# Order of the steps in the first rounds: weight split, gate split, masks, scores

## The chip, the cores and the metric

The kernel runs on one core of a Trainium2 chip. The metric is the device time of one execution in microseconds (us), the median of several runs. PE is TensorE, DVE is VectorE, ACT is ScalarE, POOL is GpSimd, SP is SyncE, which issues most DMAs here.

## The reference

A linear attention with per-channel decay over r, k, v of shape (4, 8, 768, 48) gives x of shape (3072, 384). On x stands a mixture of 8 experts, whose gate is balanced by 8 rounds of row and column normalisation, and whose outputs are summed densely.

```python
for t in range(S):                                   # attention
    cur = einsum('bhd,bhe->bhde', u * kt, vt)
    y[:, :, t] = einsum('bhd,bhde->bhe', rt, state + cur)
    state = w[..., None] * state + einsum('bhd,bhe->bhde', kt, vt)
x = y.transpose(0, 2, 1, 3).reshape(3072, 384)
P = exp(x @ w_gate - max)                            # gate, then 8 times:
P /= P.sum(1) ; P /= P.sum(0) ; P *= N / E
out = sum_e P[:, e] * (relu(x @ w1[e]) @ w2[e])
```

## The kernel before

The tokens are 24 tiles of 128. The attention takes a tile per *round* (loop over i, line 720, 27 rounds), as a pipeline: `prep(i + 2)` scales r on POOL and k on DVE by decay tables; `bonus_dot(i + 1)` forms r k u on POOL; `stage_b(i + 1)` transposes r and k on PE, with two ACT copies; `bonus(i)` is a DVE sum and two POOL products; `stage_c(i)` makes the scores pA, which DVE copies through a mask into at_ (two buffers whose masked half stays zero), and the state update pu; `stage_e(i - 2)` transposes x, which ACT has scaled, casts it to f16 on ACT and takes the f16 residue on DVE, both into hbx; `stage_d(i - 1)` multiplies the masked scores with v (py), after which DVE makes x, its maximum and a power-of-two scale; `stage_f(i - 3)` multiplies x by the split gate matrix (px). The PSUM pool ps3, tag pa, has four buffers in turn for the transposes, pA, pu and py of all these.

Every f32 operand of the experts becomes two f16 parts, a high part (ACT) and a low part, the residue (DVE). Expert 0's products (`g1_unit`, `g2_half`, in the list units) run on PE between the stages from round 5 on, by `work` at two places of a round. In rounds 0 to 4 `work` calls `spin(3)`, three matmuls on zeros, instead. Experts 1 to 7 follow after the loop.

Expert 0's weights are split in the rounds too. `split_weights` (line 151) gives a list of steps for w1 and then for w2: three maxima `amax`, `reduce_max`, an empty step, `across` (maximum over partitions by PE), an empty step, `scale`, then `high` and `low` for three chunks. `prepare()` runs the next step; STEPS (line 708) tells how many of them a round runs at its two places: the first (a) follows `stage_c`, the second (b) follows `stage_d`. The gate matrix wg is split likewise by `gate_max`, `gate_across` and `gate_split`, all three in round 2. Each engine keeps the order in which the program issues its instructions (class InOrder).

Ahead of the rounds stand the fills (hbx, at_, wbd, rp, kp), the decay tables on DVE, and an If (line 409) on a flag from DVE, whose body runs only for decays out of range. SP issues the loads in program order; the loads of v 1, r 3, k 3, wg, v 2 and v 3 stand behind the If (lines 413 to 418).

Of the kernel before, what the change touches and what calls it, by code (L numbers as in the profile page):

```python
# [8 lines left out]
F32 = mybir.dt.float32  # L9
# [3 lines left out]
ALU = mybir.AluOpType  # L13
# [19 lines left out]
def rwkv_sinkhorn_moe(  # L33
# [13 lines left out]
    V, S_, G, T, Q = (  # L47
        InOrder(tc, e) for e in (nc.vector, nc.scalar, nc.gpsimd, nc.tensor, nc.sync)
    )
# [4 lines left out]
    P = 128  # L54
# [96 lines left out]
    def split_weights(e, r1, r2, home):  # L151
        w1h = part(home, F16, 0, (KC, F))
        w1l = part(home, F16, KC * F, (KC, F))
        w2h = part(home, F16, 2 * KC * F, (FC, DM))
        w2l = part(home, F16, 2 * KC * F + FC * DM, (FC, DM))
        isw = const.tile([P, 2], F32, name=f"isw_{e}")
        sw = sm.tile([P, 2], F32, tag="sw", name=f"sw_{e}")
        m = sm.tile([P, 2 * KC], F32, tag="wm", name=f"wm_{e}")
        ma_ = [sm.tile([P, 1], F32, tag=f"wma{j}", name=f"wma_{e}_{j}") for j in range(2)]
        res = {}  # L160
        pieces = []

        def rest_():
            pass

        for raw, wh, wl, j in ((r1, w1h, w1l, 0), (r2, w2h, w2l, 1)):
            fl = [x.rearrange("p c f -> p (c f)") for x in (raw, wh, wl)]
            n = fl[0].shape[1] // KC

            def amax(i, fl=fl, j=j, n=n):  # L170
                V.tensor_reduce(
                    m[:, j * KC + i : j * KC + i + 1], fl[0][:, i * n : (i + 1) * n],
                    axis=AX.X, op=ALU.max, apply_absolute_value=True,
                )

            def reduce_max(j=j):
                V.tensor_reduce(ma_[j], m[:, j * KC : (j + 1) * KC], axis=AX.X, op=ALU.max)

            def across(j=j):
                res[j] = over_partitions(ma_[j], 1, ps1, "ph", f"w{e}_{j}")  # L180
                next(res[j])

            def scale(j=j):
                pow2_scale(next(res[j]), isw[:, j : j + 1], sw[:, j : j + 1], 0.25)

            def high(i, fl=fl, j=j, n=n):
                sl = slice(i * n, (i + 1) * n)
                S_.activation(fl[1][:, sl], fl[0][:, sl], AF.Copy, scale=sw[:, j : j + 1])

            def low(i, fl=fl, j=j, n=n):  # L190
                sl = slice(i * n, (i + 1) * n)
                V.scalar_tensor_tensor(
                    fl[2][:, sl], fl[0][:, sl], sw[:, j : j + 1], fl[1][:, sl],
                    op0=ALU.mult, op1=ALU.subtract,
                )

            steps = [lambda i=i, f=amax: f(i) for i in range(KC)] + [reduce_max, rest_, across, rest_, scale]
            for i in range(KC + 1):
                fs = [lambda i=i, f=high: f(i)] if i < KC else []
                fs += [lambda i=i, f=low: f(i - 1)] if i else []  # L200
                if i >= KC - 1:
                    fs.append(lambda i=i, j=j: split_done.add((("w1", "w2")[j], i - KC + 1)))
                steps.append(lambda fs=fs: [f() for f in fs])
            pieces += steps
        return (w1h, w1l, w2h, w2l, isw), pieces
# [113 lines left out]
    for c in range(KC):  # L319
# [11 lines left out]
    V.memset(unit[:, :, 0:1], 1.0)  # L331
    V.memset(step[:, :, 0:1], 0.0)
    V.memset(hbx[:, HB : 2 * HB], 0.0)
    S_.mul(
        hbx[:, 2 * HB :].rearrange("p (a q) -> p a q", q=HP),
        unit[:, :1, 1:].broadcast_to([P, HB // HP, HP]), 0.0,
    )
    spin(19)
    wbd = ac.tile([P, NPAIR, 2, D], F32, name="wbd")
    G.memset(wbd, 0.0)  # L340
# [11 lines left out]
    at_ = [ac.tile([P, H, C], F32, name=f"at{i}") for i in range(2)]  # L352
    for t_ in rp_ + kp_:
        G.memset(t_[:, :, D:], 0.0)
    for t_ in at_:
        G.memset(t_, 0.0)

    wlim = part(hb3, F32, 2496, (H, D))[:1]
    flag = ac.tile([1, 1], F32, name="flag")
# [51 lines left out]
            scan_channels(scratch)  # L411

    load_part(1, "v", v)
    load_part(3, "r", r)
    load_part(3, "k", k)
    Q.dma_start(wg, w_gate.rearrange("(c p) e -> p c e", p=P))
    load_part(2, "v", v)
    load_part(3, "v", v)

# [14 lines left out]
    V.tensor_tensor(tab[:, :, HP:], pw[:, :, :HP], gb, op=ALU.mult)  # L434
    V.tensor_tensor(tab[:, :, :HP], iv[:, :, HP:0:-1], gb, op=ALU.mult)
    S_.copy(tabr[:, :, :HP], pw[:, :, HP - 1 :: -1])
    S_.copy(tabr[:, :, HP:], iv[:, :, 1:])
    rtab = ac.tile([P, NPAIR, 2, HP], F32, name="rtab")
    ktab = ac.tile([P, NPAIR, 2, HP], F32, name="ktab")
# [42 lines left out]

    def bonus_dot(tt):
        ld_ = loads[tt]
        rk = at2.tile([P, H, D], F32, tag="rk", name=f"rk_{tt}", bufs=3)
        G.tensor_tensor(rk, ld_["r"], ld_["k"], op=ALU.mult)
        G.tensor_tensor(rk, rk, ub, op=ALU.mult)
        st[tt]["rk"] = rk

# [213 lines left out]
    for sg in range(3):  # L703
# [2 lines left out]
        side += steps  # L706

    STEPS = {
        0: (2, 1), 1: (1, 2), 2: (2, 1), 3: (1, 1), 4: (1, 0),
        5: (1, 1), 6: (2, 2), 7: (3, 1), 8: (1, 1),  # L710
    }

    def n_steps(i):
        return STEPS.get(i, (2, 2) if i < 22 else (3, 2))
# [3 lines left out]
    stage_b(0)  # L718
    bonus_dot(0)
    for i in range(NTT + 3):  # L720
        if i == 2:
            gate_max()
        if i + 2 < NTT:
            if i + 4 < NTT:
                load_chunk(i + 4)
            if i == 0:
                Q.dma_start(raws[1], w2[0].rearrange("(c p) d -> p c d", p=P))
            prep(i + 2)
        if i + 1 < NTT:
            bonus_dot(i + 1)  # L730
            stage_b(i + 1)
        if 2 <= i <= NTT + 1:
            scale_x(i - 2)
        work(1, i > 4)
        if i < NTT:
            bonus(i)
            if ("S", i) in st:
                st[i]["S"] = st.pop(("S", i))
            stage_c(i)
        for _ in range(n_steps(i)[0]):  # L740
            prepare()
        if i <= NTT:
            work(2 if i > 8 else 1, i > 4)
        if i == 2:
            gate_res = gate_across()
        if i >= 2:
            bank_ = ps2.tile([P, TB], F32, tag="po", name=f"px_{i}")
        if 2 <= i <= NTT + 1:
            stage_e(i - 2, bank_)
            emitted[0] = i - 1  # L750
        if i > NTT:
            work(2)
        if 1 <= i <= NTT:
            stage_d(i - 1)
        if i == 2:
            gate_split(gate_res)
        for _ in range(n_steps(i)[1]):
            prepare()
        if 3 <= i:
            stage_f(i - 3, bank_)  # L760
        done = i - 2
        if 0 <= done < NTT and done % TH == TH - 1:
            po_ = done // TH
            if po_ == 0:
                units += [g1_unit(0, fc, W) for fc in range(FC)]
                units += [g2_half(0, t, 0, W) for t in range(TH)]
                pend = [(0, t, 1) for t in range(TH)]
            for j in range(2 if po_ else 0):
                g1 = [g1_unit(po_, fc, W) for fc in range(j * FHC, (j + 1) * FHC)]
                g2 = [g2_half(*a, W) for a in pend]  # L770
                units += merged(g1, g2)
                pend = [(po_, t, j) for t in range(TH)]
# [447 lines left out]
```

## Time and profile before

| | us |
|---|---|
| median of 3 runs | 1563.85 (1563.62 to 1565.07) |
| the profiled execution | 1563.49 |
| its span, first to last instruction | 1561.8 |
| PE busy | 1549.8 |
| DVE, ACT, POOL busy | 1020.8, 671.9, 589.0 |

The granted clock of PE is 1.000 over the span. Round i of the attention can be found in the trace by PE's `stage_b`: the transposes prT of tile 5 (round 4) start at 43.53 us and the last round ends near 258 us. A busy engine is not an engine at its peak, and an average over the span says little of the first 50 us; so the rows are read round by round. In a timeline, the bracket at the end of a line tells how long the engine stood idle before it and who released it.

### The profile page before, as it was taken

How to read it: one execution, taken by the hardware profiler on the slowest of the kernel's cores; microseconds unless marked ns; L12 is line 12 of the kernel's file. 1: busy time of each engine (PE TensorE's matmuls, PEld its weight loads, DVE VectorE, ACT ScalarE, POOL GpSimd, SP SyncE). 2: the span in 40 equal slices, each digit the busy share in tenths (PEclk: the TensorE clock that was granted, in tenths of full speed). 3: DMA queues.
4: the chain of work that ended last, by engine and by line, in shares of the span. 5: the costliest groups of instructions: out<-in, count | busy, mean ns of one | idle time of the engine just before them, and what ended most of it. 6: DMA issues, size and time to landing. Idle time of an engine off the chain costs nothing.

```text
span 1561.8 us, 24068 instructions
## 1 busy us (share of the span) xinstructions
PE 1549.8 (99%) x9297; PEld 899.0 (58%) x9297; DVE 1020.8 (65%) x1694; ACT 671.9 (43%) x1190; POOL 589.0 (38%) x688
## 2 busy tenths in 40 slices
PE   8999999999999999999999999999999999999999
PEld 5877786655555555555555555555555555555555
DVE  7876674957666676666666666666666656656554
ACT  3433332534444354544444453544444444535320
POOL 8777764620012424243342424242423324242200
PEclk9999999999999999999999999999999999999999
DMA  9333311221215556576766666565545555556434
GB/s 197 68 88 79 84 49 36 98 82 45 92 64 103 79 87 111 85 127 90 128 83 122 86 127 90 93 95 70 86 57 99 57 95 61 96 59 97 56 91 132
DMA packets 167638, 138.26 MB, mean 89 GB/s; under 512 B 90337, under 2 KB 161762, under 8 KB 167522
## 3 DMA queue, kind: packets, MB, share of 16 engines
q0 software_dynamic: 44928, 61.36, 32.6%
q1 hardware_dynamic: 122384, 75.35, 17.4%
q8 instruction: 73, 1.20, 0.3%
q14 instruction: 43, 0.35, 0.1%
q10 hardware_dynamic: 210, 0.00, 0.0%
HBM read 55.39 MB, written 80.23 MB: 87 GB/s over the span
## 4 chain that ended last, share of the span: by engine, by line
PE 95%; DVE 2%; POOL 1%; ACT 0%; issue 0%; DMA 0%; SPq 0%; POOLq 0%; DVEq 0%; ACTq 0%
PE po L29 47%; PE bZ L29 11%; PE bY L29 11%; PE ph L29 5%; PE bA L29 5%; PE bB L29 5%; PE py L29 3%; PE bC L29 2%; PE pA L29 1%; PE pu L29 1%; PE px L29 1%; PE prT L29 1%; POOL rk L29 1%; PE pkT L29 1%; DVE tb L29 0%
## 5 line engine op out<-in xcount | busy, mean ns | idle before, releaser
L29 PE MATMUL po<-ws,hbx 128*128 128x384 f16 x3360 | 736.8, 326 | 0.0
L29 POOL DMA_DIRECT2D accd<-stg x288 | 249.7, 867 | 695.4 <-ACT stg L29 681.1
L29 PEld LDWEIGHTS <-hbx 128*128 128x128 f16 x3504 | 336.3, 98 | 292.7 <-issue 1.3
L29 PEld LDWEIGHTS <-ws 128*128 128x128 f16 x3096 | 302.4, 98 | 243.8 <-issue 1.4
L29 ACT ACTIVATE hbx<-tb 128x512 f16<-128x512 f32 x224 | 141.0, 630 | 450.0 <-DVE tb L29 450.0
L29 PE MATMUL po<-ws,hb 128*128 128x384 f16 x1248 | 322.8, 326 | 0.0
L29 DVE TENSOR_TENSOR tb<-bY,tb 128x512 f32<-128x512 f32 x168 | 116.1, 691 | 195.6 <-PE bY L29 195.4
L29 ACT ACTIVATE stg<-po,pe 128x384 f32<-128x384 f32 x312 | 179.1, 574 | 121.8 <-PE po L29 94.9
L29 PE MATMUL bZ<-xv,ws 128*128 128x512 f16 x840 | 227.0, 379 | 0.4 <-DVE tb L29 0.4
L29 PE MATMUL bY<-xv,ws 128*128 128x512 f16 x840 | 227.0, 379 | 0.0
L29 DVE TENSOR_TENSOR tb<-bZ,tb 128x512 f32<-128x512 f32 x168 | 115.5, 688 | 136.0 <-PE bZ L29 136.0
L29 PEld LDWEIGHTS <-hb 128*128 128x128 f16 x1248 | 121.9, 98 | 93.0
L29 POOL TENSOR_TENSOR ucb<-rawb 128x256 f32<-128x256 f32 x84 | 75.8, 953 | 118.0 <-DMA rawb<-in_moe_w_dram 118.0
L29 DVE TENSOR_TENSOR tb<-bB,tb 128x512 f32<-128x512 f32 x112 | 77.4, 691 | 49.2 <-PE bB L29 47.3
L29 PE MATMUL ph<-hbx,ws 128*128 128x384 f16 x576 | 104.3, 326 | 0.5 <-DVE hb L29 0.5
L29 DVE SCALAR_TENSOR_TENSOR hb<-tb,hbx 128x512 f16<-128x512 f32 x112 | 77.2, 689 | 24.6 <-ACT hbx L29 19.5
L29 PE MATMUL bA<-xv,ws 128*128 128x512 f16 x336 | 90.8, 379 | 0.0
L29 PE MATMUL bB<-xv,ws 128*128 128x512 f16 x336 | 90.8, 379 | 0.0
L29 DVE SCALAR_TENSOR_TENSOR hbx<-tb,hbx 128x512 f16<-128x512 f32 x112 | 77.9, 695 | 14.7 <-ACT hbx L29 10.4
L29 DVE SCALAR_TENSOR_TENSOR hb<-ph,hb 128x384 f16<-128x384 f32 x64 | 35.3, 553 | 40.7 <-ACT hb L29 40.5
L29 ACT COPY tb<-bZ 128x512 f32<-128x512 f32 x56 | 32.7, 585 | 65.6 <-PE bZ L29 65.6
L29 ACT ACTIVATE hb<-ph 128x384 f16<-128x384 f32 x64 | 31.2, 489 | 59.7 <-PE ph L29 58.7
(165 smaller groups left out, 1613.7 us busy)
## 6 DMA issues: line engine op xcount, KB each, us to landing
accd<-stg POOLq DMA_DIRECT2D x288, 192.0 KB, 3.7
rawb<-in_moe_w_dram SPq DMA_DIRECT2D x28, 768.0 KB, 7.1
e0d<-stg SPq DMA_DIRECT2D x48, 192.0 KB, 1.9
hb<-e0d SPq DMA_DIRECT2D x48, 192.0 KB, 3.7
rn<-in_r_dram SPq DMA_DIRECT2D x24, 192.0 KB, 3.2
kn<-in_k_dram SPq DMA_DIRECT2D x24, 192.0 KB, 3.6
vn<-in_v_dram SPq DMA_DIRECT2D x24, 192.0 KB, 2.8
accd<-stg SPq DMA_DIRECT2D x24, 192.0 KB, 1.8
```

Of the source, the lines that this page charges most:

```text
L29: return lambda *a, **k: self.tc.keep_in_program_order(f(*a, **k))
```

## The change

The weight steps are cut anew: two highs stand alone, and each further high comes two steps ahead of its low (14 steps per matrix instead of 12), with other numbers in STEPS. `gate_max` and `gate_across` move from round 2 to round 1, `gate_split` from the end of round 2 to behind its `stage_c`, and wg's load from behind r 3 and k 3 to ahead of them. The two buffers of at_ are filled by ACT (a broadcast multiply by zero, as one part of hbx already was) instead of POOL: the first behind the fill of hbx, the second between the two copies of the table tabr. POOL's product r k of tile 0 (rk0) is issued ahead of the If. In round 0, `stage_b(1)` follows `stage_c(0)` instead of preceding it.

```diff
--- before.py
+++ after.py
@@ -195,11 +195,15 @@
                 )
 
             steps = [lambda i=i, f=amax: f(i) for i in range(KC)] + [reduce_max, rest_, across, rest_, scale]
-            for i in range(KC + 1):
-                fs = [lambda i=i, f=high: f(i)] if i < KC else []
-                fs += [lambda i=i, f=low: f(i - 1)] if i else []
-                if i >= KC - 1:
-                    fs.append(lambda i=i, j=j: split_done.add((("w1", "w2")[j], i - KC + 1)))
+
+            steps += [lambda i=i, f=high: f(i) for i in range(2)]
+            for i in range(KC):
+                fs = [lambda i=i, f=high: f(i + 2)] if i + 2 < KC else []
+                if fs:
+                    steps.append(lambda fs=fs: fs[0]())
+                fs = [lambda i=i, f=low: f(i)]
+                if i:
+                    fs.append(lambda i=i, j=j: split_done.add((("w1", "w2")[j], i - 1)))
                 steps.append(lambda fs=fs: [f() for f in fs])
             pieces += steps
         return (w1h, w1l, w2h, w2l, isw), pieces
@@ -331,10 +335,15 @@
     V.memset(unit[:, :, 0:1], 1.0)
     V.memset(step[:, :, 0:1], 0.0)
     V.memset(hbx[:, HB : 2 * HB], 0.0)
-    S_.mul(
-        hbx[:, 2 * HB :].rearrange("p (a q) -> p a q", q=HP),
-        unit[:, :1, 1:].broadcast_to([P, HB // HP, HP]), 0.0,
-    )
+
+    def fill(x_):
+        n = x_.shape[1]
+        S_.mul(
+            x_.rearrange("p (a q) -> p a q", q=HP),
+            unit[:, :1, 1:].broadcast_to([P, n // HP, HP]), 0.0,
+        )
+
+    fill(hbx[:, 2 * HB :])
     spin(19)
     wbd = ac.tile([P, NPAIR, 2, D], F32, name="wbd")
     G.memset(wbd, 0.0)
@@ -352,8 +361,10 @@
     at_ = [ac.tile([P, H, C], F32, name=f"at{i}") for i in range(2)]
     for t_ in rp_ + kp_:
         G.memset(t_[:, :, D:], 0.0)
-    for t_ in at_:
-        G.memset(t_, 0.0)
+    fill(at_[0].rearrange("p h c -> p (h c)"))
+
+    rk0 = at2.tile([P, H, D], F32, tag="rk", name="rk_0", bufs=3)
+    G.tensor_tensor(rk0, loads[0]["r"], loads[0]["k"], op=ALU.mult)
 
     wlim = part(hb3, F32, 2496, (H, D))[:1]
     flag = ac.tile([1, 1], F32, name="flag")
@@ -411,9 +422,9 @@
             scan_channels(scratch)
 
     load_part(1, "v", v)
+    Q.dma_start(wg, w_gate.rearrange("(c p) e -> p c e", p=P))
     load_part(3, "r", r)
     load_part(3, "k", k)
-    Q.dma_start(wg, w_gate.rearrange("(c p) e -> p c e", p=P))
     load_part(2, "v", v)
     load_part(3, "v", v)
 
@@ -434,6 +445,7 @@
     V.tensor_tensor(tab[:, :, HP:], pw[:, :, :HP], gb, op=ALU.mult)
     V.tensor_tensor(tab[:, :, :HP], iv[:, :, HP:0:-1], gb, op=ALU.mult)
     S_.copy(tabr[:, :, :HP], pw[:, :, HP - 1 :: -1])
+    fill(at_[1].rearrange("p h c -> p (h c)"))
     S_.copy(tabr[:, :, HP:], iv[:, :, 1:])
     rtab = ac.tile([P, NPAIR, 2, HP], F32, name="rtab")
     ktab = ac.tile([P, NPAIR, 2, HP], F32, name="ktab")
@@ -482,8 +494,10 @@
 
     def bonus_dot(tt):
         ld_ = loads[tt]
-        rk = at2.tile([P, H, D], F32, tag="rk", name=f"rk_{tt}", bufs=3)
-        G.tensor_tensor(rk, ld_["r"], ld_["k"], op=ALU.mult)
+        rk = rk0
+        if tt:
+            rk = at2.tile([P, H, D], F32, tag="rk", name=f"rk_{tt}", bufs=3)
+            G.tensor_tensor(rk, ld_["r"], ld_["k"], op=ALU.mult)
         G.tensor_tensor(rk, rk, ub, op=ALU.mult)
         st[tt]["rk"] = rk
 
@@ -706,8 +720,8 @@
         side += steps
 
     STEPS = {
-        0: (2, 1), 1: (1, 2), 2: (2, 1), 3: (1, 1), 4: (1, 0),
-        5: (1, 1), 6: (2, 2), 7: (3, 1), 8: (1, 1),
+        0: (2, 1), 1: (1, 2), 2: (4, 2), 3: (1, 1), 4: (0, 1),
+        5: (1, 1), 6: (1, 2), 7: (4, 2), 8: (1, 1),
     }
 
     def n_steps(i):
@@ -718,7 +732,7 @@
     stage_b(0)
     bonus_dot(0)
     for i in range(NTT + 3):
-        if i == 2:
+        if i == 1:
             gate_max()
         if i + 2 < NTT:
             if i + 4 < NTT:
@@ -728,6 +742,7 @@
             prep(i + 2)
         if i + 1 < NTT:
             bonus_dot(i + 1)
+        if i + 1 < NTT and i:
             stage_b(i + 1)
         if 2 <= i <= NTT + 1:
             scale_x(i - 2)
@@ -737,11 +752,15 @@
             if ("S", i) in st:
                 st[i]["S"] = st.pop(("S", i))
             stage_c(i)
+        if i == 2:
+            gate_split(gate_res)
+        if i == 0:
+            stage_b(1)
         for _ in range(n_steps(i)[0]):
             prepare()
         if i <= NTT:
             work(2 if i > 8 else 1, i > 4)
-        if i == 2:
+        if i == 1:
             gate_res = gate_across()
         if i >= 2:
             bank_ = ps2.tile([P, TB], F32, tag="po", name=f"px_{i}")
@@ -752,8 +771,6 @@
             work(2)
         if 1 <= i <= NTT:
             stage_d(i - 1)
-        if i == 2:
-            gate_split(gate_res)
         for _ in range(n_steps(i)[1]):
             prepare()
         if 3 <= i:

```

## Rows read from the trace of the kernel before

**Rows 1.** The page's table of busy time: engine, busy us, share, instructions.

```profile
PE 1549.8 (99%) x9297; PEld 899.0 (58%) x9297; DVE 1020.8 (65%) x1694; ACT 671.9 (43%) x1190; POOL 589.0 (38%) x688
```

**Rows 2.** PE's waits, 13 to 79 us: engine, tile, releaser, total us, times, longest.

```profile
PE pu L29 <- ACT rT L29: 1.6, 1, 1.6
PE px L29 <- DVE hbx L29: 1.1, 2, 0.8
PE prT L29 <- POOL rp L29: 0.6, 2, 0.5
PE pmax_w L29 <- DVE wma L29: 0.4, 1, 0.4
```

**Rows 3.** Timeline of PE: start us, us, engine, operation, count, [idle before <-releaser].

```profile
16.77 1.16 PE L29 MATMUL pA<-rT,kT 64*128 64x128 f32 x16
...
38.82 1.13 PE L29 MATMUL pu<-vn,kp 128*128 128x96 f32 x8 [1.59 <-ACT rT L29]
...
43.38 0.29 PE L29 MATMUL px<-wgp,hbx 128*128 128x16 f16 x6
...
51.80 0.29 PE L29 MATMUL px<-wgp,hbx 128*128 128x16 f16 x6 [0.81 <-DVE hbx L29]
...
78.19 0.29 PE L29 MATMUL px<-wgp,hbx 128*128 128x16 f16 x6 [0.31 <-DVE hbx L29]
```

**Rows 4.** Timeline of POOL, 0 to 50 us.

```profile
5.90 1.84 POOL L29 MEMSET at<- 128x1024 f32 x2
...
14.97 1.31 POOL L29 TENSOR_TENSOR rk<-rn,kn 128x384 f32<-128x384 f32 x1
```

**Rows 5.** Timeline of ACT, round 7.

```profile
75.56 1.15 ACT L29 ACTIVATE ws<-ws,sw 128x1024 f16<-128x1024 f32 x1 [3.22 <-DVE sw L29]
...
76.61 0.47 ACT L29 ACTIVATE hb<-ph 128x384 f16<-128x384 f32 x1
```

**Rows 6.** Timeline of DVE, around the If.

```profile
6.98 0.78 DVE L29 TENSOR_SCALAR wsafe<-wt 128x4 f32<-128x4 f32 x1 [0.75 <-DVE flag L29]
```

**Rows 7.** Timeline of DVE, rounds 0 to 4.

```profile
17.58 0.55 DVE L29 TENSOR_REDUCE dg<-rk 128x8 f32<-128x384 f32 x1 [0.90 <-POOL rk L29]
...
23.13 0.68 DVE L29 TENSOR_TENSOR kp<-kn,ktab 128x384 f32<-128x384 f32 x1
...
30.63 0.53 DVE L29 TENSOR_TENSOR S<-pu,S 128x384 f32<-128x384 f32 x1
...
31.52 0.26 DVE L29 TENSOR_REDUCE mt_wg<-pmax_wg 1x1 f32<-1x128 f32 x1
...
34.28 0.56 DVE L29 TENSOR_TENSOR hbx<-px,hbx 128x384 f16<-128x384 f32 x1 [2.26 <-ACT hbx L29]
...
36.38 0.14 DVE L29 TENSOR_SCALAR iswg<-pmax_wg 128x1 f32<-128x1 f32 x1
...
37.65 0.55 DVE L29 TENSOR_TENSOR kp<-kn,ktab 128x384 f32<-128x384 f32 x1
...
40.53 1.27 DVE L29 SCALAR_TENSOR_TENSOR ws<-ws,sw,ws 128x1024 f16<-128x1024 f32 x1
...
43.58 0.56 DVE L29 TENSOR_TENSOR x<-py,rk 128x384 f32<-128x384 f32 x1 [1.30 <-PE py L29]
...
49.84 1.45 DVE L29 SCALAR_TENSOR_TENSOR ws<-ws,sw,ws 128x1024 f16<-128x1024 f32 x1
```

**Rows 8.** Timeline of SP's queue: start of issue, us of issue.

```profile
16.99 0.51 SPq L29 DMA_DIRECT2D rn<-in_r_dram  x1
...
18.40 0.70 SPq L29 DMA_DIRECT2D wg<-in_moe_w_gate_dram  x1
```

**Rows 9.** DMA issues by line: KB each, median us from issue to landing.

```profile
rn<-in_r_dram SPq DMA_DIRECT2D x1, 192.0 KB, 4.9
...
wg<-in_moe_w_gate_dram SPq DMA_DIRECT2D x1, 12.0 KB, 4.5
```

**Rows 10.** Timeline of ACT, round 2.

```profile
33.77 0.48 ACT L29 CAST hbx<-px 128x384 f16<-128x384 f32 x1 [5.33 <-POOL rk L29]
```


## The prediction

> **What bounds the kernel now.** I read the page's busy table first. TensorE (PE) is busy 1549.8 of 1561.8 us [rows 1], so 12 us is all that an edit that removes no matmul can return. The second view is the list of PE's waits between 13 and 79 us, the only stretch in which the edited steps run before PE's own queue hides everything: four waits, 1.6, 1.1, 0.6 and 0.4 us, 3.7 us together [rows 2]. What is left lies ahead of 13 us (the table chain of DVE, which the change touches only indirectly) and behind 79 us (nothing edited is there: rounds from 9 on call the same steps in the same places). The matmuls and the idle-filling `spin` calls keep their number. So the question is how many of those 3.7 us close, and whether a new wait opens.
>
> A wait that closes early counts only if nothing later gives it back. The reader should therefore follow three instructions of PE: f(0), the first gate product at 43.38; f(1) at 51.80, which comes after 0.81 us of waiting for DVE; and f(4) at 78.19, after 0.31 us for DVE [rows 3]. Each `stage_f(t)` waits for `stage_e(t+1)`'s VectorE residue when both lie in the same group of three tiles (their ranges in hbx interleave), which is what these releasers show.
>
> **The change part by part.** *Steps.* Per weight matrix `split_weights` gives 14 steps, where it gave 12: two highs alone, then high, low, low, low. STEPS sums to 3, 3, 6, 2, 1, 2, 3, 6, 2 (28) against 3, 3, 3, 2, 1, 2, 4, 4, 2 (24). So w1's lows leave DVE in rounds 2b, 3a, 3b (2b: second place of round 2) where they were in 3a, 3b, 4a; the amax steps of w2 move to 4b, 5a, 5b; w2's scale and its first **two** highs stand together in 7a, ahead of that round's second unit; its lows stay in 7b, 8a, 8b. Everything ends in round 8 as before, so g2 units and later token steps keep their rounds.
>
> *Masks and rk0.* POOL's two fills of at_ (1.84 us from 5.90) and the product rk of tile 0 (1.31 us at 14.97) leave POOL's stretch that follows the tables; rk0 runs in POOL's idle time ahead of the If [rows 4]. ScalarE takes two fills of about 1.15 us each (its high of the same 128x1024 size [rows 5]), the first behind its hbx fill, the second between its two table copies, where it stands idle; cost nothing, cover DVE's scan and reciprocal; uncovered, 1.15 us each. The row that bears on more: DVE's `wsafe`, 128x4, took 0.78 us at 6.98 and ended at 7.76, just as POOL's fills ended at 7.74 [rows 4, 6]. A DVE operation on one column takes 0.14 in this trace [rows 7], so up to 0.64 us of the front may be bought. The Trainium skill has the mechanism (SBUF — State Buffer, "Who interferes with whom"): a DVE operation in a two-port mode and a GpSimd instruction share one port pair, and whoever comes second waits for the other's end. By that rule the front shrinks by 0.64 us if rk0 is through by then; without it, by nothing; the two times agree with the rule. I put this in a rival, since what follows is pinned by loads.
>
> *Scores ahead of second transposes.* pA of tile 0 started at 16.77 behind the transposes of tile 1, which had waited for POOL [rows 2, 3]. It now needs only kT of tile 0, so it starts about 1.2 us earlier, and DVE's dg of tile 0, which waited 0.90 us for POOL's rk chain [rows 7], no longer does. DVE has no gap from 17.58 to 32.02 (its next idle, 2.26 us, ends at 34.28) [rows 7], so its list moves forward by 0.88: kp of tile 3, old 23.13, is ready at 22.25.
>
> *Load order.* That kp needs k of tile 3, and now wg (0.70 us of issue) goes out ahead of r and k of tile 3 instead of behind them [rows 8]. The r load took 4.9 us to land, wg 4.5 with a sixteenth of the bytes [rows 9], so r landed at 21.9 and wg at 22.9. The same loads in another order should end no later than 22.9; the delay of kp is between 0 and 0.65 us. I take 0, since k goes second to last as before, behind 12 KB more, and keep 0.65 for the range. The rule against it (DMA: Bandwidth & Descriptors, "Why small descriptors are slow (HBM only)") charges a fixed overhead to each descriptor, and wg's rows are 32 bytes long. By it wg would cost its followers more than its bytes; that it took as long as 192 KB agrees, and it is the other end's mechanism. Gate_max now stands on DVE's queue ahead of kp; wg issued near 17.0 lands at 21.5 by its 4.5, ahead of 22.2, so it costs nothing unless wg is over 0.7 us later.
>
> *Gate a round sooner, round 2.* From kp's start to S of tile 2 is 7.50 us; the gate's maximum pair, which ran behind S (31.52 to 32.02, 0.50), now lies ahead [rows 7]. So S starts at 22.25 + 7.50 + 0.46 = 30.2. Behind it stand S itself (0.46), the gate's split (36.38 to 37.65, 1.27, in which DVE also waits for ScalarE once) and w1's three scale operations (0.43: from S to the maximum pair is 0.89) [rows 7]: w1's scale is there at 32.4. Now ScalarE issues high 0 and high 1, 1.05 us apart as in round 7's rows [rows 5], and only then the cast of tile 0's transposed x at 34.5; it was at 33.77, held by POOL [rows 10]. POOL's release comes about a microsecond earlier but no longer decides. The cast releases DVE's residue 0.51 later, at 35.0 where it was 34.28: **0.7 us later**, and DVE stands idle 2.6 us in place of 2.26. From there DVE is unbroken: residue and x of tile 1 2.10, low 0 1.2, kp to S of tile 3 2.88, low 1 1.2, residue of tile 1 0.55 [rows 7], sum 7.93, done at 42.95. So f(0) is at 43.0, 0.4 us ahead of 43.38 (0.25 behind it with the late kp). PE's old 1.6 us wait in front of pu [rows 2, 3] shrinks to about 0.8, since ScalarE has wgp and high 0 out of the way earlier but x of tile 1, whose buffer pA needs, is late; and part of the rest reappears in front of f(0).
>
> *Round 4.* f(1) waited 0.81 us because low 2 (1.45) stood ahead of tile 2's residue [rows 3, 7]. It is gone from there. PE needs 51.80 - 0.81 - 43.38 = 7.61 from f(0) to f(1); DVE from x of tile 2 to the residue 49.84 - 43.58 = 6.26 plus 0.55, less than that, so PE is not held: f(1) at 50.6, **1.2 us ahead** (0.55 with the late kp).
>
> *Round 5 and 6.* DVE gets one amax (about 1.2) into 4b and loses one from 6a; it had gaps ahead of x in both, and I cost it at nothing; uncovered it would delay f(3) by under 0.3.
>
> *Round 7.* ScalarE's queue was: high 0 at 75.56, the relu of the unit at 76.61 [rows 5], the cast, and behind them DVE's residue, for which PE waited 0.31 [rows 3]. The start at 75.56 hangs on DVE's S of that round, which follows PE, so it moves with the lead. A second high ahead of the relu adds 1.05, all of it on that path, since PE waits there already: f(4) at 78.19 - 1.2 + 1.05 = 78.04. So **1.05 of the 1.2 us are given back**, and the net is -0.15 us; with the late kp +0.5. I take -0.1.
>
> **The sum** is made against the profiled execution, 1563.49 us (span 1561.8, and 1.7 around it); the median of the runs, 1563.85, is 0.36 above it. 1563.85 - 0.1 = 1563.75, written 1563.8.
>
> **The rivals.**
> *Front and loads (faster).* The 0.64 us of `wsafe` come through and k of tile 3 lands by 21.6, so that kp moves too: net -0.8, 1563.0. For: the two end times that agree. Against: r landed at 21.9 when nothing was ahead of it, and SP's queue is not moved forward.
> *No give-back (faster).* In round 7 ScalarE gets the scale earlier, or DVE's release isn't the end of that wait: the 1.2 us stay, 1562.6; with the front, 1562.0. Against: the 0.31 us wait shows that there is no slack. All four waits closed and the front too, 3.7 + 0.64, would give 1559.5; that needs every rival gain at once.
> *The double high ahead of the relu and the cast (slower).* It costs 1.05 in round 7 and 0.7 in round 2 in any case; it decides as soon as the lead at f(1) is under 1.05. With k late by 0.65 the net is +0.5; with wg holding it 1 us longer and the slower low (1.45) the lead is gone and the net is +1.05 to +1.7: 1564.9 to 1565.5. For: wg's 4.5 us. Against: the lead needs only 0.81 from round 4, which is sure.
> *Nothing arrives* (the same instructions in other places, waits trading places): 1563.85, inside the forecast.
>
> **How the numbers follow.** Forecast, 1563.2 to 1564.4: 0.47. Front and loads: 0.20. No give-back: 0.12. All waits closed, below 1561: 0.05. Double high with a late k, 1564.4 to 1565.5: 0.16. Range 1562.0 to 1565.3. A measurement of this kernel can tell about 0.2%, 3.1 us, from no change; only the case with all waits closed gets there on the fast side, and on the slow side only a stall that no row shows. Faster 0.07, same 0.89, slower 0.04.
>
> **What would show it.** In the changed trace: `wsafe` at 0.14 us; kp of tile 3 near 22.3; ScalarE with two highs in a row ahead of the cast at 34.5; f(0) near 43.0 with a wait for DVE; f(1) near 50.6 with none; f(4) near 78.0 with a wait of about 1.3 us. Wrong would be: kp of tile 3 waiting for its load beyond 23, or f(4) as far ahead as f(1).

## The result, and the profile after

The changed kernel took 1568.11 us (median of 20 runs, 1566.69 to 1569.16) against 1564.05 of the kernel before in the same series: ratio 1.0022, 95% interval 1.0016 to 1.0028. It is slower by 3.4 us by that ratio and by 4.1 between the medians, where 1563.8 had been forecast. The profiled execution has a span of 1566.7 us against 1561.8, so 4.9 us are to be found in it. One thing is needed for reading the times: those of the kernel before lie in two groups, near 1563.7 and near 1565.8 (2 of these 20 near 1567.5), and a median moves with their shares; what the groups are comes out below (e13).

PE's waits between 13 and 90 us, the answer to [rows 2]: the 1.6 us in front of pu is gone, as is one of the two for POOL; the wait for the weight maximum has grown from 0.4 to 1.7, that in front of the gate products (px) from 1.1 to 3.2.

```profile
PE px L29 <- DVE hbx L29: 3.2, 2, 1.8
PE pmax_w L29 <- DVE wma L29: 1.7, 1, 1.7
```

The timeline of PE, the answer to [rows 3]:

```profile
14.98 1.16 PE L29 MATMUL pA<-rT,kT 64*128 64x128 f32 x16
...
26.66 0.27 PE L29 MATMUL pmax_w<-ident,wma 128*1 128x128 f32 x1 [1.73 <-DVE wma L29]
...
29.44 1.75 PE L29 MATMUL pA<-rT,kT 64*128 64x128 f32 x16
...
46.15 0.37 PE L29 MATMUL px<-wgp,hbx 128*128 128x16 f16 x6 [1.81 <-DVE hbx L29]
...
53.67 0.29 PE L29 MATMUL px<-wgp,hbx 128*128 128x16 f16 x6
...
81.15 0.29 PE L29 MATMUL px<-wgp,hbx 128*128 128x16 f16 x6 [1.35 <-DVE hbx L29]
...
82.49 3.02 PE L29 MATMUL ph<-hbx,ws 128*128 128x384 f16 x9
```

Four places where the two executions can be laid side by side tell where the time came from. (f(0) is the px at 46.15, f(1) at 53.67, f(4) at 81.15; f(5) follows at 91.91, and stood at 87.27 before.)

| | before | after | later by |
|---|---|---|---|
| f(0) | 43.38 | 46.15 | 2.77 |
| f(1) | 51.80 | 53.67 | 1.87 |
| f(4) | 78.19 | 81.15 | 2.96 |
| f(5) | 87.27 | 91.91 | 4.64 |
| span | 1561.8 | 1566.7 | 4.9 |

So all but 0.3 us lies ahead of 92 us: 1.9 us up to round 4, 1.1 more up to f(4), and 1.7 more just behind f(4), where PE waits for nothing. That last piece is in the durations: nine matmuls `ph` take 3.02 us at 82.49, where nine take 1.63 or 1.64 elsewhere, as in the kernel before:

```profile
79.25 1.63 PE L29 MATMUL ph<-hbx,ws 128*128 128x384 f16 x9
```

The scores at 29.44 take 1.75 instead of 1.16. The view by stretches (columns: stretch, length, busy us and count of PE, weight loads, DVE, ACT and POOL, granted clock of PE, DMA share, GB/s) shows why:

```profile
28.00:29.00 1.00, 1.00 (x5) 0.30 (x2) 0.86 (x6) 0.70 (x3) 1.00 (x2) 0.50 0.87 265
81.00:82.00 1.00, 0.85 (x12) 0.85 (x12) 0.97 (x3) 0.49 (x2) 0.36 (x1) 0.95 0.91 185
82.00:83.00 1.00, 1.00 (x6) 0.74 (x5) 0.90 (x5) 0.77 (x2) 0.92 (x2) 0.50 0.12 28
85.00:86.00 1.00, 1.00 (x12) 0.56 (x11) 0.17 (x1) 0.45 (x1) 0.00 (x0) 0.84 0.74 143
```

Twice the granted clock falls to 0.50, which is the lower of the two levels, 1.2 GHz, for some 3.4 us, each time soon after PE had stood idle: 1.73 us ahead of 26.66 and 1.35 us ahead of 81.15 (the first and the last bracket of PE's timeline above). In the first of them PE's list from prT of tile 3 to the start of pu takes 4.35 us (26.77 to 31.12) and took 2.73 in the same round before (26.19 to 28.92); in the second its list from prT to the start of pA takes 4.14 (81.30 to 85.44), before 2.47 (78.34 to 80.81). So each costs PE 1.6 to 1.7 us. The profile of before had no such stretch; its granted clock is 1.000 over the span.

DVE, the answer to [rows 6] and [rows 7]:

```profile
6.98 0.17 DVE L29 TENSOR_SCALAR wsafe<-wt 128x4 f32<-128x4 f32 x1 [0.75 <-DVE flag L29]
...
16.21 0.55 DVE L29 TENSOR_REDUCE dg<-rk 128x8 f32<-128x384 f32 x1 [0.15 <-DVEq L420]
...
22.09 0.18 DVE L29 TENSOR_REDUCE wgm<-wg 128x1 f32<-128x24 f32 x1 [0.22 <-DMA wg<-in_moe_w_gate_dram]
...
23.82 0.58 DVE L29 TENSOR_TENSOR kp<-kn,ktab 128x384 f32<-128x384 f32 x1 [1.55 <-DMA kn<-in_k_dram]
...
31.22 1.35 DVE L29 COPY_PREDICATED at<-mask,pA 128x512 f32<-128x512 int32 x2 [1.18 <-PE pA L29]
...
37.45 0.56 DVE L29 TENSOR_TENSOR hbx<-px,hbx 128x384 f16<-128x384 f32 x1 [2.62 <-ACT hbx L29]
...
40.74 1.35 DVE L29 TENSOR_TENSOR kp<-kn,ktab 128x384 f32<-128x384 f32 x1
...
44.17 1.45 DVE L29 SCALAR_TENSOR_TENSOR ws<-ws,sw,ws 128x1024 f16<-128x1024 f32 x1
...
45.55 0.55 DVE L29 TENSOR_TENSOR hbx<-px,hbx 128x384 f16<-128x384 f32 x1
```

`wsafe` takes 0.17 us. DVE is ready for kp of tile 3 at 22.27, waits 1.55 us for its load and starts it at 23.82; PE's longer wait for the weight maximum is the end of that list. SP's queue, the answer to [rows 8], shows why the load is late: v 1, the first load behind the If, is issued at 17.71 (16.49 before), and r 3, which came second at 16.99 before, at 18.84.

```profile
17.71 0.38 SPq L29 DMA_DIRECT2D vn<-in_v_dram  x1
...
18.14 0.58 SPq L29 DMA_DIRECT2D wg<-in_moe_w_gate_dram  x1
...
18.84 0.41 SPq L29 DMA_DIRECT2D rn<-in_r_dram  x1
...
19.34 0.52 SPq L29 DMA_DIRECT2D kn<-in_k_dram  x1
```

ACT, the answer to [rows 5] and [rows 10]: two highs in a row (count x2) stand ahead of the cast at 36.97 and ahead of the relu at 79.58.

```profile
34.87 2.19 ACT L29 ACTIVATE ws<-ws,sw 128x1024 f16<-128x1024 f32 x2 [1.06 <-DVE sw L29]
...
36.97 0.46 ACT L29 CAST hbx<-px 128x384 f16<-128x384 f32 x1
```

```profile
77.48 2.19 ACT L29 ACTIVATE ws<-ws,sw 128x1024 f16<-128x1024 f32 x2 [3.23 <-DVE sw L29]
...
79.58 0.47 ACT L29 ACTIVATE hb<-ph 128x384 f16<-128x384 f32 x1
```

### The profile page after: what moved, and what is told of

It is laid out like the page before. It is cut to its first block, busy times and chain, and to the rows that moved or that the text cites. A ratio compares the mean times of both kernels' runs of the same rounds, so it can differ in the third digit from the quotient of the medians.

```text
span 1566.7 us, 24067 instructions
## 1 busy us (share of the span) xinstructions
PE 1553.4 (99%) x9297; PEld 900.8 (57%) x9297; DVE 1021.6 (65%) x1694; ACT 674.8 (43%) x1192; POOL 588.0 (38%) x686
## 4 chain that ended last, share of the span: by engine, by line
PE 95%; DVE 3%; ACT 0%; issue 0%; DMA 0%; POOL 0%; ACTq 0%; DVEq 0%; POOLq 0%
PE po L29 47%; PE bZ L29 11%; PE bY L29 11%; PE ph L29 5%; PE bA L29 5%; PE bB L29 5%; PE py L29 3%; PE bC L29 2%; PE pA L29 1%; PE pu L29 1%; PE px L29 1%; PE prT L29 1%; PE pkT L29 1%; DVE at L29 0%; DMA kn<-in_k_dram 0%
```

## Experiments

The theories were: **A**, the new weight steps put two highs ahead of a cast (round 2) and of a relu (round 7) that PE waits for; **B** and **C**, the late loads behind the If come from the fills and rk0, or from wg's new place; **D**, a gap of PE can be followed by a stretch at the lower clock, which has a price of its own. The times of all runs (e1 to e4, e5 to e8, e9 to e12, e13 and e14 each beside runs of the kernel before on the same chip):

| run | median us (lowest to highest) | before | ratio, 95% interval |
|---|---|---|---|
| e1 one high in 7a | 1565.76 (1564.92 to 1566.80) | 1564.06 | 1.0009 (0.9999 to 1.0019) |
| e2 fills and rk0 only | 1564.15 (1563.13 to 1565.39) | 1564.06 | 1.0000 (0.9991 to 1.0010) |
| e3 weight steps only | 1565.90 (1564.14 to 1566.36) | 1564.06 | 1.0005 (0.9995 to 1.0014) |
| e4 gate and load order only | 1562.68 (1561.73 to 1564.78) | 1564.06 | 0.9990 (0.9981 to 1.0000) |
| e5 all but the weight steps | 1562.89 (1561.91 to 1564.50) | 1565.46 | 0.9991 (0.9981 to 1.0000) |
| e6 one high in 2a and 7a | 1564.41 (1563.00 to 1566.05) | 1565.46 | 0.9997 (0.9988 to 1.0007) |
| e7 scores only | 1563.89 (1563.54 to 1567.17) | 1565.46 | 0.9997 (0.9987 to 1.0006) |
| e8 the changed kernel again | 1568.92 (one run) | 1565.46 | |
| e9 one high each, lows late | 1563.18 (1561.99 to 1564.36) | 1564.38 | 0.9989 (0.9980 to 0.9999) |
| e10 before, spin(24) | 1564.58 (1563.52 to 1567.74) | 1564.38 | 1.0004 (0.9994 to 1.0013) |
| e11 changed, gaps filled | 1565.57 (1564.68 to 1566.26) | 1564.38 | 1.0004 (0.9995 to 1.0014) |
| e12 as e5, wg ahead of w1 | 1563.22 (1561.86 to 1563.87) | 1564.38 | 0.9988 (0.9979 to 0.9998) |
| e13 before, gaps filled | 1564.02 (1563.49 to 1564.64) | 1564.14 | 0.9997 (0.9987 to 1.0007) |
| e14 as e5, gaps filled | 1562.20 (1561.64 to 1562.93) | 1564.14 | 0.9984 (0.9974 to 0.9993) |

**e1, one high in round 7a.** On the changed kernel:

```diff
-        5: (1, 1), 6: (1, 2), 7: (4, 2), 8: (1, 1),
+        5: (1, 1), 6: (1, 2), 7: (3, 3), 8: (1, 1),
```

> The changed kernel with STEPS 7: (3, 3), so that only one high of w2 stands ahead of round 7's second unit; all else as changed. Theory A (two highs ahead of the relu open a 1.35 us wait of PE in front of f(4), and the half-speed stretch of 3.4 us behind it costs 1.7 more): the wait falls to 0.3, no half-speed stretch at 82 us, 1568.1 - 1.05 - 1.7 = 1565.4. Rival (the wait is given back later, or the half-speed stretch comes from elsewhere): 1567 to 1568, with the clock at half speed near 82 us as before.

Measured 1565.76, which is 2.35 less than the 1568.11 of the changed kernel (2.0 by the ratios); 2.7 had been expected. The wait in front of f(4) is back at 0.31, and no stretch at the lower clock is near it:

```profile
80.33 0.29 PE L29 MATMUL px<-wgp,hbx 128*128 128x16 f16 x6 [0.31 <-DVE hbx L29]
```

In this execution such stretches lie at 12 to 16 us and at 46 to 50, behind the gap ahead of the tables (2.2 us) and behind the 1.81 us in front of f(0). PE's list from f(0) to f(1) takes 9.09 us here, with such a stretch in it, and 7.52 in the profile of the changed kernel, which has none there: 1.6 us once more. The second high of round 7a is shown to cost some 2.0 to 2.4 us, its 1.04 us of waiting and the stretch behind it together.

**e2, fills and rk0 only,** the diff's hunks on `fill` and `rk0` on the kernel before.

> The kernel before with the fills on ScalarE and rk0 ahead of the If, nothing else. Theory B (the late loads behind the If, v 1 issued at 17.71 instead of 16.49, come from this part, whose earlier DMA or POOL work holds SP): v 1 again near 17.7, wsafe 0.17 us, tables 0.6 earlier, and a kernel about as fast as before or up to 1.5 us slower. Rival (the late exit of SP from the If has nothing to do with it and differs from run to run or from program to program): v 1 near 16.5, 1563.3 to 1564.

v 1 is issued at 16.36, so theory B isn't borne out: with this part in, SP left the If early (e8 says more). `wsafe` takes 0.17 us and the first kp starts at 12.54 (13.16 before): the front is 0.6 us shorter. Nothing of it arrives, since kp of tile 3 still starts at 23.13. No load holds it there: DVE, 1.36 us early at dg (16.22), waits 1.27 us for pA, which in the old order stands behind the transposes of tile 1 and which PE reaches after a stretch at the lower clock (12 to 16 us).

```profile
6.98 0.17 DVE L29 TENSOR_SCALAR wsafe<-wt 128x4 f32<-128x4 f32 x1 [0.74 <-DVE flag L29]
...
12.54 3.52 DVE L29 TENSOR_TENSOR kp<-kn,ktab 128x384 f32<-128x384 f32 x3 [1.22 <-ACT ktab L29]
...
18.04 1.36 DVE L29 COPY_PREDICATED at<-mask,pA 128x512 f32<-128x512 int32 x2 [1.27 <-PE pA L29]
...
23.13 1.11 DVE L29 TENSOR_TENSOR kp<-kn,ktab 128x384 f32<-128x384 f32 x1
```

**e3, weight steps only,** the diff's hunks on `split_weights` and STEPS on the kernel before.

> The kernel before with the new weight steps and STEPS alone. Theory A: a wait of about 1.4 us in front of f(4) in round 7 and a half-speed stretch of some 3.4 us behind it, 0.8 gained in round 4: 1564.05 - 0.8 + 1.05 + 1.7 = 1566.0. Rival (the split is harmless, all loss is in rounds 1 and 2): 1563.5 to 1564.5, no half-speed stretch.

Measured 1565.90, as theory A had it. f(0) has no wait, f(1) is 0.5 us ahead of before, f(4) 0.6 behind, with the same wait as the whole change, and PE's clock falls behind it:

```profile
51.33 0.29 PE L29 MATMUL px<-wgp,hbx 128*128 128x16 f16 x6
...
78.83 0.29 PE L29 MATMUL px<-wgp,hbx 128*128 128x16 f16 x6 [1.35 <-DVE hbx L29]
```

```profile
80.00:81.00 1.00, 1.00 (x5) 0.48 (x4) 0.93 (x4) 1.00 (x3) 0.92 (x2) 0.50 0.00 0
```

**e4, gate and load order only.**

> The kernel before with wg's load ahead of r 3 and k 3 and the gate's three steps a round sooner, nothing else. Theory C (the load order is what makes DVE wait for k of tile 3 and PE for the weight maximum in round 1): kp of tile 3 waits about 0.8 us for its load, PE waits about 1 us in front of the weight maximum, perhaps with a half-speed stretch behind it: 1564.5 to 1566. Rival (the order costs nothing, the wait came only from SP's late exit from the If): no wait over 0.5 us in round 1, 1563 to 1564.

Neither theory had it right: it gains. f(0) is at 42.35 and f(4) at 77.16, 1.03 us ahead of before, and the time is 1562.68 against 1564.06. PE waits 0.7 us for the weight maximum, less than C expected, and kp of tile 3 doesn't wait for its load. ScalarE's wgp now runs at 32.56, while it would wait for POOL anyway, and the rT copy of round 3 at 35.72 instead of 38.20, so pu of round 3, which hangs on that copy, has no wait (it had 1.59, [rows 3]).

**e5, everything but the weight steps,** the changed kernel with `split_weights` and STEPS of before.

> The changed kernel with the weight steps and STEPS of before; gate, load order, fills, rk0 and scores as changed. Theory A (the loss is the split, in round 2 by two highs ahead of the cast and in round 7 by two ahead of the relu; the gate part alone gains 1.4): f(0) near 42.3, f(1) near 50.7 after 0.8 of waiting, f(4) near 77.1 after 0.3, 1562.0 to 1562.9. Rival (the loss needs the late loads of the reordered queue together with the earlier front): a wait of PE over 1 us in round 1 and 1564 or more.

1562.89, as theory A had it, though SP left the If later here than in any other profile (v 1 at 18.03) and kp of tile 3 started at 24.32. So with the old steps the late load costs little (f(0) at 42.49, still 0.89 us ahead of before), and what the change loses comes with the weight steps: 1568.11 - 1562.89 = 5.2 us.

But the weight steps alone cost the kernel before 1.8 us only (e3), and e2, e3 and e4 together add up to +0.1 + 1.8 - 1.4 = +0.5 us, where the whole change costs 4.1. So by the medians most of the loss comes where parts meet; its size is rough, with intervals of some 1.5 us to either side on each. One such meeting is in round 2. With DVE's S of tile 2 at 30.95 in e3 and at 30.98 in e1, w1's scale (isw) follows at once in e3, whereas in e1 the gate's split stands between them; so the two highs end, and the residue of tile 0 starts, 1.5 us later:

```profile
31.41 0.14 DVE L29 TENSOR_SCALAR isw<-pmax_w 128x1 f32<-128x1 f32 x1
...
34.65 0.56 DVE L29 TENSOR_TENSOR hbx<-px,hbx 128x384 f16<-128x384 f32 x1 [2.30 <-ACT hbx L29]
```

```profile
33.01 0.14 DVE L29 TENSOR_SCALAR isw<-pmax_w 128x1 f32<-128x1 f32 x1
...
36.16 0.56 DVE L29 TENSOR_TENSOR hbx<-px,hbx 128x384 f16<-128x384 f32 x1 [2.62 <-ACT hbx L29]
```

(The first pair is e3, the second e1.)

**e6, one high in 2a as well.**

```diff
-        0: (2, 1), 1: (1, 2), 2: (4, 2), 3: (1, 1), 4: (0, 1),
-        5: (1, 1), 6: (1, 2), 7: (4, 2), 8: (1, 1),
+        0: (2, 1), 1: (1, 2), 2: (3, 3), 3: (1, 1), 4: (0, 1),
+        5: (1, 1), 6: (1, 2), 7: (3, 3), 8: (1, 1),
```

> The changed kernel with STEPS 2: (3, 3) and 7: (3, 3), so that one high of w1 instead of two stands ahead of round 2's cast, and one of w2 ahead of round 7's relu. Theory A: the residue of tile 0 comes 1.05 us earlier than with round 7 alone mended (36.16 there), the wait of 1.8 us in front of f(0) falls to about 0.8, and the half-speed stretch behind it may go: 1565.76 - 1.05 = 1564.7, or 1563.0 without the stretch. Rival (DVE's three lows, one of them in round 2, are what delays f(0), whatever ScalarE does): the wait stays over 1.5 us, 1565.5.

1564.41, which is 1.35 less than e1. The wait in front of f(0) fell to 1.40 only, between what theory A and the rival had expected. In the profile f(0) is no earlier than in e1 (44.98 and 44.85): kp of tile 3 came 0.36 us later, and a stretch at the lower clock (26 to 30 us) made DVE wait 1.04 us for pA. So the gain rests on the times, and part of the rival holds: DVE's low 0, now ahead of tile 5's kp, keeps f(0) waiting (e9).

**e7, scores only.**

> The kernel before with stage_b(1) behind stage_c(0) in round 0, nothing else. Expected by every theory: within 0.4 us of before, 1563.6 to 1564.4, since kp of tile 3 waits for its load anyway. If it is over 1565, the order of PE in round 0 is part of the loss.

1563.89; f(0) at 43.40, f(4) at 78.22, as before. This edit does nothing that can be seen in the times.

**e8, the changed kernel again.**

> The changed kernel once more, for a second profile. If the late exit of SP from the If (v 1 issued at 17.71) and the half-speed stretch at 27 to 31 us belong to this program, both are there again; if they differ from execution to execution, v 1 is issued somewhere between 16.3 and 17.7 and the stretch may lie elsewhere, as in the single-part kernels, where it lay at 12 to 16 us. The waits in front of f(0) (1.8) and f(4) (1.35) stay in either case.

v 1 is issued at 16.75: the exit from the If differs by a microsecond from one execution of the same program to the next. The waits in front of f(0) and f(4) are the same (1.81, 1.34). The lower clock lies elsewhere, at 11 to 15 us and from 45 to 52, and this time there is none behind f(4), where f(5) follows 9.08 us later as before. PE's list from f(0) to f(1), with nearly 7 us at the lower clock in it, takes 10.28 us instead of 7.52. The sum is much the same, f(5) at 92.58 (91.91).

```profile
45.79 0.37 PE L29 MATMUL px<-wgp,hbx 128*128 128x16 f16 x6 [1.81 <-DVE hbx L29]
...
56.07 0.29 PE L29 MATMUL px<-wgp,hbx 128*128 128x16 f16 x6
...
83.50 0.29 PE L29 MATMUL px<-wgp,hbx 128*128 128x16 f16 x6 [1.34 <-DVE hbx L29]
...
92.58 0.30 PE L29 MATMUL px<-wgp,hbx 128*128 128x16 f16 x6
```

**e9, one high each and the lows where they were.** Against e6:

```diff
-        0: (2, 1), 1: (1, 2), 2: (3, 3), 3: (1, 1), 4: (0, 1),
+        0: (2, 1), 1: (1, 2), 2: (3, 2), 3: (1, 1), 4: (1, 1),
```

> The changed kernel with STEPS 2: (3, 2), 3: (1, 1), 4: (1, 1), 7: (3, 3): one high ahead of each cast and relu, and the lows of w1 where they were before (rounds 3a, 3b, 4a). Theory A (with the highs apart, what is left of the loss, 1.5 us against the kernel without the new steps, is low 0 in round 2, which pushes DVE's list in front of f(0)): the wait in front of f(0) goes from 1.40 to under 0.2, about 0.8 comes back in front of f(1), 1562.6 to 1563.2. Rival (the late load of k 3 alone makes that wait): it stays over 1 us, 1564.4.

1563.18, 1.2 less than e6. f(0) no longer waits, and 0.89 us are back in front of f(1), although kp of tile 3 waited 1.67 us for its load here:

```profile
42.83 0.30 PE L29 MATMUL px<-wgp,hbx 128*128 128x16 f16 x6
```

```profile
51.33 0.29 PE L29 MATMUL px<-wgp,hbx 128*128 128x16 f16 x6 [0.89 <-DVE hbx L29]
```

With e1 and e6 this takes the 5.2 us of the weight steps apart: 2.35 for the second high of 7a, 1.35 for that of 2a, 1.2 for the lows a place or two earlier, and 0.3 that these runs don't resolve. By the ratios to the kernel before the same steps are 2.0, 1.9, 1.3 and -0.3. (The intervals are some 1.5 us wide to either side, so the sizes are rough; the waits in the traces bear out the first and the third, while for the second there are only the times.)

**e10, spin(24) in the kernel before.**

> The kernel before with spin(24) in place of spin(19): five more matmuls on zeros in the gap of 2 us in which PE waits for the tables. Theory D (a gap of PE can be followed by 3 to 4 us at half speed; the two groups of times of the kernel before, near 1563.8 and near 1565.8, are executions without and with such a stretch, here behind the table gap): the gap is under 0.6 us, the upper group thins out, median 1563.5 to 1563.9. Rival (the two groups have another cause): the same two groups in the same shares, median 1564 to 1565.5.

The two groups stay (five runs below 1564.1, five above 1565.1), as the rival had it. The gap ahead of the tables was only shortened, from 2.07 to 1.15 us in the profiles, so this run alone doesn't clear it.

**e11, the changed kernel with its gaps filled.** Matmuls on zeros where PE waits; nothing waits for their results.

```diff
-    spin(19)
+    spin(22)
...
             stage_d(i - 1)
+        if i == 1:
+            spin(4)
         for _ in range(n_steps(i)[1]):
             prepare()
+        if i in (3, 7):
+            spin(6 if i == 3 else 5)
         if 3 <= i:
             stage_f(i - 3, bank_)
```

> The changed kernel with matmuls on zeros put where PE waits: 3 more ahead of the tables, 4 behind py in round 1, 6 ahead of f(0) in round 3, 5 ahead of f(4) in round 7. No wait gets shorter by that. Theory D: PE has no gap over 0.8 us, the half-speed stretches go, and with them the two times 1.7 us: 1564.6 to 1565.2. Rival (the stretches have nothing to do with the gaps, or cost nothing): 1567.5 to 1568.5.

1565.57, 2.5 less than the changed kernel (2.8 by the ratios), with nothing but idle time filled; the slowest of the ten runs, 1566.26, is faster than the fastest of the twenty of the changed kernel, 1566.69. f(0) and f(4) are still released by DVE (44.73 and 79.73), which itself comes as early as in e1, since no stretch lies in rounds 1 and 2; and behind both the clock is 1.00:

```profile
79.73 0.29 PE L29 MATMUL px<-wgp,hbx 128*128 128x16 f16 x6 [0.26 <-DVE hbx L29]
```

```profile
44.00:48.00 4.00, 3.48 (x36) 2.52 (x35) 3.86 (x9) 1.69 (x3) 3.92 (x4) 1.00 0.26 51
80.00:84.00 4.00, 4.00 (x40) 3.10 (x39) 3.86 (x9) 2.12 (x5) 3.04 (x2) 1.00 0.59 117
```

One stretch is left, at 10 to 15 us, behind the 2.18 us ahead of the tables, which the three matmuls didn't close. That the lower clock comes with PE's gaps, and that it costs some 2.5 of the 4.1 us between the two medians, is shown by this run.

**e12, wg ahead of w1,** on the kernel of e5, with spin(22).

> The kernel without the new weight steps (gate, fills, rk0, scores as changed), with wg's load ahead of w1's, so that only v 1 stands ahead of r 3 and k 3 behind the If, and spin(22). Theory C (the order wg, r 3, k 3 costs about 0.6 us at kp of tile 3): kp 0.6 earlier than with the same exit from the If, the wait in front of the weight maximum under 0.4; with fewer half-speed stretches in front 1561.5 to 1562.5, faster than 1562.9. Rival (SP's exit from the If decides alone): 1562.5 to 1563.2.

kp of tile 3 starts 6.37 us after v 1's issue (23.64 and 17.27); with wg ahead of r 3 it was 6.11 (the changed kernel), 6.91 (e8), 6.29 (e5). kp waited 1.69 us for its load and PE 1.77 us for the weight maximum, where under 0.4 had been expected, and a stretch at the lower clock followed (26 to 30 us).

```profile
23.64 0.80 DVE L29 TENSOR_TENSOR kp<-kn,ktab 128x384 f32<-128x384 f32 x1 [1.69 <-DMA kn<-in_k_dram]
```

Theory C fell as well: kp follows the moment at which SP leaves the If, and wg's place in the queue doesn't show. 1563.22 is no faster than e5.

**e13, the kernel before with its gaps filled:** five matmuls more ahead of the tables, six ahead of pu in round 3, three ahead of f(1).

> The kernel before with matmuls on zeros in its gaps of PE: 5 more ahead of the tables, 6 ahead of pu in round 3 (gap 1.59), 3 ahead of f(1) in round 4 (gap 0.81). Theory D (the upper group of times of the kernel before, near 1565.8, is executions with a half-speed stretch behind one of these gaps): the upper group is gone, median 1563.5 to 1563.9. Rival (the groups have another cause, behind the first 80 us): both groups stay, median between 1563.6 and 1565.5 as the shares fall.

The upper group is gone: 10 runs between 1563.49 and 1564.64, where 7 of the 19 runs of the kernel before beside them lie at 1565.62 and above. The mean granted clock of every run is on record, and it parts the groups: of the 106 runs of the kernel before beside e1 to e14, the 44 at 1565.46 and above all have 0.998, the 62 below 1564.5 all have 0.999 or 1.000. (In the profiles 0.999 goes with one stretch of 3.4 us, 0.998 with two.) At a share of 44 in 106 ten runs without the upper group would come by chance about once in 200 times. So the upper group is executions with more time at the lower clock. That a stretch lies behind the 1.59 or the 0.81 us gap is argued from e13 and not seen, since no profile of such an execution was taken; the gap ahead of the tables doesn't make the group by itself, for e13's profile still has 2.17 us there:

```profile
11.39 1.06 PE L29 MATMUL pt_tab<-ident,hb 128*128 128x128 f32 x8 [2.17 <-DVE wc L29]
```

Two runs of e13 have 0.998 as well and still lie at 1564.07 and 1564.25, so the lower clock can also fall where it costs little.

**e14, the kernel of e5 with its gaps filled:** three matmuls more ahead of the tables, four behind py in round 1, three ahead of f(1).

> The kernel without the new weight steps (gate, load order, fills, rk0 and scores as changed), with matmuls on zeros in PE's gaps: 3 more ahead of the tables, 4 behind py in round 1, 3 ahead of f(1) in round 4. Theory D: f(0) near 42.4, f(4) near 77.2 or earlier, no half-speed stretch behind 16 us, 1561.9 to 1562.6, the fastest of the series. Rival (what gaps and stretches cost here lies ahead of work that waits anyway): 1562.7 to 1563.2, as without the filling.

1562.20, the fastest of the series, ratio 0.9984: f(0) at 41.94, f(5) at 86.05, and no stretch at the lower clock behind 15 us. It is faster than the kernel before by 2.5 us (1.1 to 4.1), and so than the changed one. The gain over e5 (0.7 between the medians) is not clear of the noise.

## Why the prediction was wrong

**The front: right.** `wsafe` went from 0.78 to 0.17 us and the tables came 0.6 us earlier. The trace agrees with the Trainium skill (SBUF — State Buffer, "Who interferes with whom"), by which a DVE operation in a two-port mode is held up by a GpSimd operation on the shared ports: 0.78 or 0.79 with the fills on POOL in every profile, 0.17 to 0.26 without. That this operation ran in such a mode no run here shows. In the changed kernel the gain ends at the load of k 3, as forecast; in e2 it ended at pA.

**Scores ahead of second transposes: right in place, worth nothing alone** (pA at 14.98, dg at 16.21; e7). That DVE is ready for kp at 22.27, where 22.25 had been forecast, is partly luck: DVE was 1.37 us ahead at dg, where 0.88 had been reckoned without the front, and lost 0.5 of that by kp, most of it to wg's load and the gate's maximum, which had been put at nothing.

**Load order: wrong.** "The same loads in another order should end no later than 22.9" took the moment at which SP leaves the If in one execution for a fixed one. Over the 16 profiles v 1's issue runs from 16.36 to 18.03 us; the profile of before had nearly the earliest. kp of tile 3, put at 22.25 to 22.9, started at 23.35 to 24.32 wherever its load held it. wg's place doesn't show in these runs (e12). By the Trainium skill (DMA: Bandwidth & Descriptors, "Why small descriptors are slow (HBM only)") wg's 32-byte rows would cost its followers more than their bytes; no run here shows it. Half of the 1.22 us at v 1 is SP's own issue of the three loads of w1 ahead of the If, which ended at 10.58 before and at 11.18 here; the other half is the way from there through the If (5.91 and 6.53 us). Why either differs was not tried.

```profile
7.32 3.26 SPq L29 DMA_DIRECT2D ws<-in_moe_w_dram  x3
```

```profile
7.62 3.56 SPq L29 DMA_DIRECT2D ws<-in_moe_w_dram  x3
```

(The first line is the kernel before, the second the changed one.)

**Round 2, up to the residue: right in size.** From kp of tile 3 to the residue of tile 0 the sum had 35.0 - 22.25 = 12.75 us. e1, where no stretch of lower clock lies between, has 36.16 - 23.35 = 12.81. In the profiled execution it is 13.63, because DVE waited 1.18 us for pA, which PE was doing at the lower clock.

**Round 2 to f(0): under-sized.** From that residue to the end of the next one I had 7.93 us; it took 8.65 (37.45 to 46.10). The missing 0.7 is the piece from kp of tile 5 to the end of S, priced with the old rows at 2.88 and now 3.43, and low 1, 1.38 instead of 1.2. kp takes 1.35 at 40.74, where it took 0.55: it starts right after low 0, while POOL's product at 39.64 takes 2.04 instead of 0.99 at 36.69 in the kernel before:

```profile
39.64 2.04 POOL L29 TENSOR_TENSOR rk<-rk,ub 128x384 f32<-128x384 f32 x1
```

```profile
36.69 0.99 POOL L29 TENSOR_TENSOR rk<-rk,ub 128x384 f32<-128x384 f32 x1
```

By the Trainium skill (SBUF — State Buffer, "Who interferes with whom") a DVE operation with two inputs from SBUF contends with a GpSimd operation that reads SBUF, and these durations agree. I had used that section for the front only, and moved low 0 to another neighbour at its old price. The lead of 0.4 us at f(0) became a wait of 1.81 (a wait was forecast there, but not its size).

**Round 4: right.** f(1) has no wait any more, and PE takes 7.52 us from f(0) to f(1) (7.6 forecast).

**Round 7: right as a wait, wrong as a price.** The second high makes the wait 1.35 us; about 1.3 had been forecast. But the sum took a wait of PE for its own length, and here 1.7 us at the lower clock followed it.

**The steps that failed.** With the measured terms beside those of the sum the chain closes: 23.82 + 13.63 + 8.65 = 46.10, and f(0) is at 46.15. The miss at f(5), 4.8 us, is accounted for:

| | in the sum | measured | missed by |
|---|---|---|---|
| kp of tile 3 starts | 22.25 | 23.82 | 1.57 |
| from there to the residue of tile 0 | 12.75 | 13.63 | 0.88 |
| DVE's list from there to f(0) | 7.93 | 8.65 | 0.72 |
| f(0) to f(1) | 7.6 | 7.52 | -0.08 |
| f(1) to f(4) | 27.44 | 27.48 | 0.04 |
| f(4) to f(5), as before | 9.08 | 10.76 | 1.68 |

The largest part, 0.88 + 1.68 = 2.6 us, is a term that the sum put at nothing without a reason: that a wait of PE costs what it lasts, in round 7 ("1.05, all of it on that path") as in front of the weight maximum, whose wait of 1.73 us wasn't forecast either. That came from a profile in which all gaps stood at full clock. With the gaps filled the same schedule takes 2.5 us less (e11). The other 2.3 us are the delay of kp, of which I wrote "I take 0", and DVE's list ahead of f(0) at its old prices.

**The rival** on the slow side, two highs ahead of the cast and of the relu, was the right mechanism, and its point, a lead under 1.05 us at f(1), was passed (f(1) is 1.87 late). Its price, 1.05 to 1.7, had the lead gone but not turned into a delay (f(4) is 2.96 late), and left out the lower clock behind the waits that it makes, so it ended at 1565.5 instead of 1568.1. The delay of 0.7 us in round 2, which stands under the gate's heading, is neither the gate's nor the highs' alone: the residue of tile 0 starts at 34.26 in e4, at 34.65 in e3 (where kp of tile 3 came 0.46 us late) and at 34.28 in the kernel before. By itself the gate part gains 1.0 us at f(0) (e4).

## What to carry to other kernels

Where TensorE sets the end and stands at full clock, look at every gap that an edit may open, and price it with what can follow it, not with its length; filling gaps that couldn't be closed with matmuls on zeros was worth 2.5 us in the changed kernel. A step moved to another place meets other queue neighbours: two copies "ahead of time" on ScalarE were in front of the one cast that everybody waited for, and a VectorE operation beside a new GpSimd neighbour had another price. Parts that cost or gain little alone can cost much together (e3 and e4 against the whole), so try them also in pairs. A moment that a branch or a load decides is worth a second profile before a sum is built on it.

## What the runs showed of the hardware

A gap of PE was followed by 3.4 us at 1.2 GHz in some executions and not in others with the same gap: 1.81 us in front of f(0) was not followed by it in the changed kernel's first profile and was in e1 and e8 (there for 6.8 us), and 1.35 in front of f(4) was in the first profile and e3, and not in e8. The 1.59 us of the kernel before stood at full clock in its profile. Ahead of the tables 2.16 us were followed by it in e2, and 2.17 in e13 were not. A stretch of 3.4 us cost PE 1.6 to 1.7 us where it had work to do. The first load behind an If whose body doesn't run was issued anywhere from 16.36 to 18.03 us, 1 us apart for one and the same program (17.71, 16.75); from the issue of the last load ahead of the If it took 5.6 to 6.1 us in 14 of the 16 profiles, 6.5 in the first of the changed kernel and 6.8 in e5.
